# 64-token attention chunks from the fourth window on with reordered queues, and a first pair with one table set

## Chip, cores, metric

One core of a Trainium2 chip. The metric is the device time of a whole execution in microseconds (us). The profiler's span, from the first to the last instruction, is about 1.7 us shorter than the time of the same run in most runs, and all moments below are counted from the start of the span. Most executions agree within about 1%; runs marked slow (over 1.5% above the fastest of the same kernel) are left out of the ratios.

## The reference

A decayed linear attention over 64-token blocks, and behind it a layer norm, a two-layer MLP and a residual. B = 4, H = 8, S = 768, D = 64; the MLP is 512 to 2048 to 512.

```python
for b in range(nb):                       # 12 blocks of 64 tokens
    intra = einsum('bhic,bhjc->bhij', qb, kb) * Dmask
    intra = einsum('bhij,bhjd->bhid', intra, vb)
    inter = einsum('bhid,bhde->bhie', qb * lam_pow, kv_state)
    out[:, :, sl] = intra + inter
    kv_state = lam_block * kv_state + einsum('bhsd,bhse->bhde', kb * rev_pow, vb)
# ... x = out as (B, S, 512)
xn = (x - mean) / sqrt(var + 1e-6) * g_ln
out = x + relu(xn @ w_ch1) @ w_ch2
```

## The kernel before

The work is cut into 12 windows of 256 tokens (3 stretches of the sequence by 4 batches), numbered 0 to 11. A window gives the MLP two tiles of 128 tokens, one "group". The order of issue is written by hand: `plan` is the list of MLP steps (eight first-layer and eight second-layer steps for each group), and `add(n, ...)` hangs pieces of attention, of preparation and of transfers behind step n. SyncE (SP) issues the loads, the stores and the transposes by DMA, all in one queue. POOL (GpSimd) prepares K, Q and V of each window (`p0`) and decays the state.

Windows below LB use 128-token chunks, those from LB on use 64-token chunks, with less arithmetic. The two layouts differ in how a load is cut: two neighbouring tokens are 512 contiguous bytes, one token is 256.

```python
LB = 6

def source(src, u, hs):                   # u < LB: packets of 512 B, one DMA
    return src[b, hs, cc * W:(cc + 1) * W, :].rearrange("h (p j) d -> p h (j d)", j=2)
def fill(got, name, u, hs):               # u >= LB: packets of 256 B, two DMAs
    for j in range(2):
        nc.sync.dma_start(got[:, hs, j * D:(j + 1) * D],
                          src[b, hs, cc * W + j * C:..., :].rearrange("h p d -> p h d"))
# ...
def p0(u, k_eng=None):                    # preparation: POOL
    open_window(u)
    in_k(u, k_eng or nc.gpsimd)
    in_q(u, nc.gpsimd)
    in_v(u, nc.gpsimd)

def states64(u, j):                       # the state chain of a 64-token window (shortened)
    nc.vector.tensor_tensor(mid, s["pk"][0][:, j], old, op=ALU.add)     # Smid, VectorE
    nc.vector.tensor_tensor(tmp, s["pk"][1][:, j], mid, op=ALU.add)     # Stmp, VectorE
    decay(nc.gpsimd, Sn, tmp)                                           # Sn, POOL
    nc.gpsimd.tensor_copy(Sm, mid)                                      # Sm, POOL

def X(u):                                 # end of window u-1, front of window u (shortened)
    av64(u - 1); inter(u - 1, 0); kv64(u); scores64(u); inter(u - 1, 1)
    states64(u, 0); mask64(u, 0); states64(u, 1)
    norm(u - 1, 0); norm(u - 1, 1); mask64(u, 1)
# ...
add(12, (s4, 2), (p4, 2), (p0, 3, nc.vector), (transpose_dma, 3))
add(25, (s1, 3)); add(27, (s2, 3)); add(29, (s3, 3)); add(30, (s4, 3), (p4, 3))
for n, name in zip((30, 31, 32), "kqv"):
    add(n, (load_one, 6, name))
add(38, (s1, 4))
add(39, (p0, 6))                          # preparation of window 6, before ...
# ...
add(50, (s1, 5), (rstd_of, 4))            # ... window 5's state
```

`norm(u)` leaves the input xc of the MLP, and `p4(u)` has it transposed by DMA into xT; the group of window u starts on TensorE when xT is there.

## Time and profile before

| | before |
|---|---|
| time, median of 3 runs | 215.92 us (214.59 to 216.27) |
| span, granted TensorE clock | 214.9 us, 0.996 |
| starts of groups 2, 3, 4, 5, 6 on TensorE | 55.02, 72.02, 89.93, 106.11, 121.47 us |

The prediction below shows the page, the windows and the chain. What it does not show, and what decided the case, is the order of POOL's work around window 6. The timeline of POOL of the kernel before; its columns are start, duration, engine and line, operation, output <- inputs with their sizes, count, and in brackets the idle time just before with what ended it:

```profile
74.00 0.61 POOL L287 TENSOR_TENSOR Sn<-Stmp,lam_s 128x256 bf16<-128x256 f32 x1 [5.34 <-DVE Stmp L291]
...
75.70 1.16 POOL L199 CAST kq<-kin 128x512 bf16<-128x512 f32 x2
77.58 2.23 POOL L210 TENSOR_TENSOR kq<-qin,lam_p 128x512 bf16<-128x512 f32 x2 [0.72 <-DMA qin<-in_q_dram]
80.48 1.90 POOL L216 TENSOR_TENSOR vb<-vin,lam_p 128x1024 bf16<-128x1024 f32 x1 [0.67 <-DMA vin<-in_v_dram]
87.22 0.61 POOL L287 TENSOR_TENSOR Sn<-Stmp,lam_s 128x256 bf16<-128x256 f32 x1 [4.85 <-DVE Stmp L291]
```

At 74.00 POOL decays a state of window 4, from 75.70 to 82.4 it prepares window 6, whose loads are there (it waits 0.72 us for Q and 0.67 us for V), and at 87.22 it decays a state of window 5. So the order that will matter, window 6's preparation ahead of window 5's decays, is already in this kernel. POOL comes 4.85 us early to the last line. It has room, but only because window 6's loads are early.

### The profile page before, as it was taken

The page shows a single profiled execution, that of the slowest core. Times are in us where ns is not written, and L with a number is a line of the kernel's source. Part 1 is how long each engine was busy: PE and PEld are TensorE (multiplying, and loading weights), DVE is VectorE, ACT ScalarE, POOL GpSimd, SP SyncE. Part 2 cuts the span into 40 slices and gives each one's busy share as a digit, 9 for nine tenths or more (in the row PEclk, how much of TensorE's full clock was granted, in tenths as well). Part 3 has the DMA queues.
Part 4 walks back from the last instruction along what each step waited for, and adds up shares of the span by engine and source line. Part 5 has one row for each costly group of instructions (what it writes and reads, how often), then busy time and mean ns, then how long its engine had stood idle before and what let it go on. Part 6 is the DMA issues. An engine that isn't in the chain of part 4 may idle for free.

```text
span 214.9 us, 6642 instructions
## 1 busy us (share of the span) xinstructions
PE 201.9 (94%) x2884; PEld 138.2 (64%) x2899; DVE 102.9 (48%) x225; ACT 87.1 (41%) x165; POOL 79.4 (37%) x111
## 2 busy tenths in 40 slices
PE   2989999999799999999999999999999999999992
PEld 0568788454674675585585685784784874866861
DVE  3678461565168436747347256174183292522011
ACT  4765679120442244055063162261370460731600
POOL 4747139039464173229019138056065020000000
PEclk9999999999999999999999999999999999999998
DMA  4999999999999898799799999998998511320303
GB/s 130 289 272 207 219 263 160 236 284 234 215 303 208 169 229 153 110 215 209 126 220 199 137 230 200 177 203 198 206 246 131 128 27 27 99 52 0 98 3 95
DMA packets 94142, 37.13 MB, mean 173 GB/s; under 512 B 68385, under 2 KB 91169, under 8 KB 94114
## 3 DMA queue, kind: packets, MB, share of 16 engines
q1 hardware_dynamic: 89584, 32.38, 71.4%
q0 software_dynamic: 4224, 4.19, 12.4%
q8 instruction: 22, 0.36, 0.7%
q10 hardware_dynamic: 306, 0.14, 0.3%
q14 instruction: 6, 0.05, 0.1%
HBM read 27.27 MB, written 6.29 MB: 156 GB/s over the span
## 4 chain that ended last, share of the span: by engine, by line
PE 75%; DMA 13%; POOL 4%; SPq 3%; DVE 2%; issue 1%; POOLq 0%
PE pm L484 35%; PE pm L522 30%; DMA vin<-in_v_dram 6%; DMA qin<-in_q_dram 4%; SPq L71 3%; DMA kqT<-kq 2%; POOL kq L210 2%; POOL vb L216 2%; PE pm2h L513 2%; PE po L406 1%; PE po L393 1%; PE sc L247 1%; PE po L380 1%; PE sc L327 1%; PE pm1t L496 1%
## 5 line engine op out<-in xcount | busy, mean ns | idle before, releaser
L487 ACT ACTIVATE hT<-pm 128x512 bf16<-128x512 f32 x92 | 54.9, 601 | 91.2 <-PE pm L484 91.0
L484 PE MATMUL pm<-xT,w 128*128 128x256 bf16 x736 | 86.3, 273 | 1.9 <-DMA xT<-xc 1.2
L522 PE MATMUL pm<-w,hT 128*128 128x512 bf16 x353 | 81.1, 379 | 1.0 <-issue 0.3
L484 PEld LDWEIGHTS <-w 128*128 128x128 bf16 x736 | 69.8, 98 | 13.8 <-DMA xT<-xc 1.7
L522 PEld LDWEIGHTS <-hT 128*128 128x128 bf16 x368 | 35.5, 98 | 40.0
L543 DVE SCALAR_TENSOR_TENSOR o<-pm,rstd,x 128x512 f32<-128x512 f32 x23 | 17.1, 748 | 43.5 <-PE pm L522 43.4
L287 POOL TENSOR_TENSOR Sn<-Stmp,lam_s 128x256 bf16<-128x256 f32 x16 | 9.7, 611 | 69.7 <-DVE Stmp L365 49.0
L435 DVE SCALAR_TENSOR_TENSOR xc<-po,mv,g_row 128x512 bf16<-128x512 f32 (+1 forms) x24 | 16.8, 706 | 1.8
L257 DVE TENSOR_TENSOR mA<-sc,keep 128x512 bf16<-128x512 f32 x20 | 13.1, 685 | 6.8 <-PE sc L247 6.7
L428 ACT COPY x<-po 128x512 f32<-128x512 f32 x18 | 9.9, 588 | 11.3 <-PE po L393 5.3
L430 DVE BATCH_NORM_STATS2 stats<-x 128x6 f32<-128x512 f32 x18 | 12.4, 688 | 3.9 <-ACT x L428 3.9
L417 DVE COPY seen<-po 128x8 f32<-128x8 f32 x18 | 2.3, 162 | 23.2 <-PE po L406 23.2
L216 POOL TENSOR_TENSOR vb<-vin,lam_v 128x1024 bf16<-128x1024 f32 (+1 forms) x7 | 11.8, 1696 | 3.7 <-DMA vin<-in_v_dram 3.7
L210 POOL TENSOR_TENSOR kq<-qin,lam_q 128x512 bf16<-128x512 f32 x10 | 10.3, 1045 | 7.0 <-DMA qin<-in_q_dram 7.0
L210 POOL TENSOR_TENSOR kq<-qin,lam_p 128x512 bf16<-128x512 f32 x12 | 12.3, 1042 | 0.9 <-DMA qin<-in_q_dram 0.7
L216 POOL TENSOR_TENSOR vb<-vin,lam_p 128x1024 bf16<-128x1024 f32 x6 | 11.4, 1896 | 1.7 <-DMA vin<-in_v_dram 1.7
L199 POOL CAST kq<-kin 128x512 bf16<-128x512 f32 (+1 forms) x18 | 10.3, 599 | 0.6 <-DMA kin<-in_k_dram 0.6
L333 DVE TENSOR_TENSOR mA<-sc,keep 128x512 bf16<-128x512 f32 x12 | 8.2, 681 | 1.4 <-PE sc L327 1.4
L406 PE MATMUL po<-Sn,kqT 64*64 64x64 bf16 x216 | 7.4, 199 | 0.0
L224 PE MATMUL tp<-ident,kq 128*128 128x128 bf16 x48 | 6.2, 277 | 0.3 <-ACT kq L199 0.2
L406 PEld LDWEIGHTS <-kqT 64*64 64x64 bf16 x304 | 5.3, 108 | 1.5 <-issue 1.5
L224 PEld LDWEIGHTS <-kq 128*128 128x128 bf16 x48 | 4.1, 120 | 3.2 <-DVE kq L199 1.5
(98 smaller groups left out, 146.0 us busy)
## 6 DMA issues: line engine op xcount, KB each, us to landing
out_dram<-o SPq DMA_DIRECT2D x22, 256.0 KB, 4.5
w<-in_moe_w_ch_dram POOLq DMA_DIRECT2D x8, 512.0 KB, 9.6
kin<-in_k_dram SPq DMA_DIRECT2D x14, 256.0 KB, 3.9
qin<-in_q_dram SPq DMA_DIRECT2D x14, 256.0 KB, 5.2
vin<-in_v_dram SPq DMA_DIRECT2D x14, 256.0 KB, 5.6
kin<-in_k_dram SPq DMA_DIRECT2D x5, 512.0 KB, 6.5
qin<-in_q_dram SPq DMA_DIRECT2D x5, 512.0 KB, 8.7
vin<-in_v_dram SPq DMA_DIRECT2D x5, 512.0 KB, 7.7
```

Source lines behind the costliest of these rows:

```text
L199: (eng.copy if eng is nc.scalar else eng.tensor_copy)(dst[:, :, :, j], src[:, :, :, j])
L210: eng.tensor_tensor(dst[:, :, :, j], src[:, :, :, j], lq[:, :, :, j:j + 1].to_broadcast([128, n, 2, D]), op=ALU.mult)
L216: eng.tensor_tensor(st[u]["vb"][:, hs], qkv_in[u]["v"][:, hs], lv.to_broadcast([128, n, 2, D]), op=ALU.mult)
L224: nc.tensor.transpose(tp[:, i, j, :], s["kq"][:, a, p, j], ident)
L257: nc.vector.tensor_tensor(s[f"mA{hf}"][:, e], s[f"sc{hf}"][e], kp[:, None, :, :].to_broadcast([128, 2, 2, 128]), op=ALU.mult)
L406: nc.tensor.matmul(s["po"][ab][half[jq], 2 * p + e, :], lhsT=qT[half[e], p, jq, half[ab]], rhs=s["S"][ab][jq][half[e], p, :], start=False, ...
L430: nc.vector.bn_stats(stats, po if early else x)
L435: nc.vector.scalar_tensor_tensor(xc[:, sl], in0=po[:, sl], scalar=mv[:, 0:1], in1=g_row[:, sl], op0=ALU.subtract, op1=ALU.mult)
L484: nc.tensor.matmul(pm[:, b, :], lhsT=w1[n // W2K][:, kk, (n % W2K) * 128:(n % W2K + 1) * 128], rhs=xT_of[g][:, kk, 0:N], start=(b == 0 and ...
L487: nc.scalar.activation(hT[:, u * NB:(u + 1) * NB, 0:N], pm, ACT.Relu)
L522: nc.tensor.matmul(acc[i], lhsT=hT[:, kk, i * 128:(i + 1) * 128], rhs=w2[kk // W2K][:, kk % W2K, :], start=(kk == 0), stop=(kk == KB - 1))
L543: nc.vector.scalar_tensor_tensor(o[:, ab], in0=a, scalar=rstd[:, ab:ab + 1], in1=x[:, ab], op0=ALU.mult, op1=ALU.add)
```

## The change

Three intents. Windows 3, 4 and 5 take the 64-token form too (LB from 6 to 3), so TensorE has less attention to do. The queues are reordered for that: window 4's K on another queue, its Q and V behind window 2's transposes, the stores of windows 0 to 2 taken out of the MLP's finish and issued later, K and Q transposes issued one by one. In the first pair, one table set with Ln and Exp is loaded up front, and copies and scores are moved forward.

```diff
-    LB = 6
+    LB = 3
+    nc.scalar.preload_act_table_set("natural_log_exp_and_others")
-        elif ab == 1:
-            for j in range(2):
-                nc.sync.dma_start(rows[j], o[half[j]])
+        elif ab == 1 and u > 2:
+            store(u)
     # ... first pair: order of transposes, copies and activations (cut)
+    def first64(u, ahead=None):
+        kv64(u)
+        scores64(u)
+        if ahead is not None:
+            in_q_one(ahead, nc.gpsimd, 0)
+        mask64(u, 0)
+        states64(u, 0)
+        if ahead is not None:
+            in_q_one(ahead, nc.vector, 1)
+        mask64(u, 1)
+        states64(u, 1)
     # ... the plan; the old entries of windows 3 to 5 are taken out
+    add(11, (open_window, 3), (in_k, 3, nc.scalar), (in_q, 3, nc.gpsimd))
+    add(12, (s4, 2), (make_keep64,), (in_v, 3, nc.gpsimd), (load_one, 4, "k", nc.scalar))
+    add(12, (transpose_dma, 3, 0), (to_xT, 2, 0), (transpose_dma, 3, 1), (to_xT, 2, 1))
+    add(12, (load_one, 4, "q"), (load_one, 4, "v"))
+    add(20, (open_window, 4), (in_k, 4, nc.vector))
+    add(21, (first64, 3, 4))
+    add(22, (transpose_dma, 4, 0), (transpose_dma, 4, 1), (load_one, 5, "k"), (load_one, 5, "q"))
+    add(23, (in_v, 4, nc.gpsimd))
+    add(28, (wind_up, 3), (p4, 3), (load_one, 5, "v"))
+    add(28, (open_window, 5), (in_k, 5, nc.gpsimd), (transpose_dma, 5, 0))
+    add(30, (first64, 4))
+    add(32, (in_q, 5, nc.gpsimd), (in_v, 5, nc.gpsimd))
+    add(34, (rstd_of, 3), (transpose_dma, 5, 1), (store, 0), (store, 1))
+    add(40, (store, 2))
-    for j in range(6, NU):
+    for j in range(5, NU):
         at = 55 + 16 * (j - 6)
-        if j > 6:
-            for n, name in zip((23, 21, 19), "kqv"):
+        if j > 5:
+            for n, name in zip((17, 16, 15) if j == 6 else (23, 21, 19), "kqv"):
                 add(at - n, (load_one, j, name))
             add(at - 13, (p0, j))
     # ... transposes one by one; the old entries of the block X (cut)
+        add(at + (4 if j == 5 else 2), (X, j), (p4, j - 1))
```

With j = 6, the loads of window 6 stand at steps 38 to 40 and its preparation at step 42. Window 5's block `X` stands at step 39 + 4 = 43. In the kernel before the loads stand at steps 30 to 32, the preparation at 39 and window 5's first state at 50: the change issues the loads eight steps later and the block seven steps earlier.

More of the change, by code (lines that the diff above doesn't have):

```diff
@@ L66, in source, with fill @@
         return src[b, hs, cc * W:(cc + 1) * W, :].rearrange("h (p j) d -> p h (j d)", j=2)
-    def fill(got, name, u, hs):
+    def fill(got, name, u, hs, eng=None):
+        eng = eng or nc.sync
         src = dict(k=k, q=q, v=v)[name]
         if u < LB:
-            nc.sync.dma_start(got[:, hs], source(src, u, hs))
+            eng.dma_start(got[:, hs], source(src, u, hs))
             return
@@ L74, in fill, with load_one @@
         for j in range(2):
-            nc.sync.dma_start(got[:, hs, j * D:(j + 1) * D],
-                              src[b, hs, cc * W + j * C:cc * W + (j + 1) * C, :].rearrange("h p d -> p h d"))
-    def load_one(u, name):
+            eng.dma_start(got[:, hs, j * D:(j + 1) * D],
+                          src[b, hs, cc * W + j * C:cc * W + (j + 1) * C, :].rearrange("h p d -> p h d"))
+    def load_one(u, name, eng=None):
         got = inp.tile([128, H, 2 * D], F32, tag=name + "in", name=name + "in")
-        fill(got, name, u, slice(0, H))
+        fill(got, name, u, slice(0, H), eng)
         qkv_in.setdefault(u, {})[name] = got.rearrange("p h (j d) -> p h j d", j=2)
@@ L148 @@
     nc.vector.memset(eps_t, eps)
+    nc.vector.tensor_copy(e_p[:, 0:1], io_p)
+    nc.vector.tensor_scalar(e_p[:, 1:2], e_p[:, 0:1], -1.0, None, op0=ALU.mult)
     e_q = const.tile([128, 1], F32)
@@ L211, in in_q, with in_q_one @@
                               lq[:, :, :, j:j + 1].to_broadcast([128, n, 2, D]), op=ALU.mult)
+    def in_q_one(u, eng, j):
+        src = qkv_in[u]["q"].rearrange("p (a e) j d -> p a e j d", e=2)
+        lq = lam_p[:, 0, :].rearrange("p (a e) -> p a e", e=2)
+        eng.tensor_tensor(part(1, st[u]["kq"], ALL)[:, :, :, j], src[:, :, :, j],
+                          lq[:, :, :, None].to_broadcast([128, NP, 2, D]), op=ALU.mult)
     def in_v(u, eng, hs=ALL):
@@ L225, in transpose_pe, with transpose_dma @@
         (eng.tensor_copy if eng else nc.scalar.copy)(s["kqT"][:, a, pairs[0]:pairs[0] + n], tp)
-    def transpose_dma(u):
+    def transpose_dma(u, a):
         s = st[u]
-        s["kqT"] = wk.tile([128, 2, NP, 2, 128], BF16, tag="kqT", bufs=3, name="kqT")
-        for a in range(2):
-            nc.sync.dma_start_transpose(s["kqT"][:, a].rearrange("p b j t -> p (b j) t"),
-                                        s["kq"][:, a].rearrange("p b j e d -> p (b j e d)"))
+        if "kqT" not in s:
+            s["kqT"] = wk.tile([128, 2, NP, 2, 128], BF16, tag="kqT", bufs=3, name="kqT")
+        nc.sync.dma_start_transpose(s["kqT"][:, a].rearrange("p b j t -> p (b j) t"),
+                                    s["kq"][:, a].rearrange("p b j e d -> p (b j e d)"))
     def scores(u, hf, early=False):
@@ L268, in mask_by_act, with mask_two_ways @@
             nc.vector.tensor_tensor(m, m, kp[:, None, :, :].to_broadcast([128, 2, 2, 128]), op=ALU.mult)
+    def mask_two_ways(u, hf):
+        s = st[u]
+        m = s[f"mA{hf}"][:, 1]
+        nc.scalar.copy(m, s[f"sc{hf}"][1])
+        mask(u, hf, (0,))
+        kp = keep_h.rearrange("p a b t -> p a (b t)")
+        nc.vector.tensor_tensor(m, m, kp[:, None, :, :].to_broadcast([128, 2, 2, 128]), op=ALU.mult)
     def kv(u, tag="mm"):
@@ L452, in to_xT @@
         else:
-            xt = mm_tile([128, KA, 128], BF16, "xt")
-            for kk in range(KA):
-                nc.tensor.transpose(xt[:, kk, :], s["xc"][:, ab, kk * 128:(kk + 1) * 128], ident)
-            nc.scalar.copy(dst, xt)
+            n_x = 2 if t == 0 else 1
+            for i_x in range(n_x):
+                w = KA // n_x
+                xt = mm_tile([128, w, 128], BF16, "xt")
+                for kk in range(w):
+                    at = i_x * w + kk
+                    nc.tensor.transpose(xt[:, kk, :], s["xc"][:, ab, at * 128:(at + 1) * 128], ident)
+                (nc.vector.tensor_copy if i_x else nc.scalar.copy)(dst[:, i_x * w:(i_x + 1) * w], xt)
     def rstd_of(u):
@@ L547, in finish, with store @@
                 nc.sync.dma_start(rows[j][:, ab], o[half[j], ab])
-        elif ab == 1:
-            for j in range(2):
-                nc.sync.dma_start(rows[j], o[half[j]])
+        elif ab == 1 and u > 2:
+            store(u)
+    def store(u):
+        for j in range(2):
+            nc.sync.dma_start(rows_of(u)[j], o_of[u][half[j]])
     def finish_half(t, a, z, w):
@@ L589 @@
     load_window(1)
-    in_k(0, nc.vector, HA)
-    transpose_pe(0, 0, (0, 1))
-    keep_busy(1, "po0")
     for j in range(2):
@@ L597 @@
         nc.scalar.activation(lam_s[half[e]], ln_p[half[e], :, e], ACT.Exp, scale=float(C))
+    in_k(0, nc.vector, HA)
+    transpose_pe(0, 0, (0, 1))
     nc.vector.tensor_tensor(lam_q[:, :, 1], lam_q[:, :, 0], lam_b, op=ALU.mult)
-    nc.vector.tensor_copy(e_p[:, 0:1], io_p)
-    nc.vector.tensor_scalar(e_p[:, 1:2], e_p[:, 0:1], -1.0, None, op0=ALU.mult)
-    for i in range(2):
-        nc.scalar.activation(lam_p[:, i], lnlam, ACT.Exp, scale=e_p[:, i:i + 1])
     in_q(0, nc.vector, HA)
@@ L609 @@
     transpose_pe(0, 0, (2, 3), nc.vector)
+    scores(0, 0)
+    transpose_pe(0, 1, (2, 3))
     nc.scalar.copy(g_row, g_all)
-    transpose_pe(0, 1, (2, 3))
+    for i in range(2):
+        nc.scalar.activation(lam_p[:, i], lnlam, ACT.Exp, scale=e_p[:, i:i + 1])
     sqrt_first = const.tile([128, 1], F32)
@@ L614 @@
     in_v(0, nc.gpsimd, HB)
-    scores(0, 0)
     mask(0, 0)
     scores(0, 1, early=True)
-    mask_by_act(0, 1)
+    mask_two_ways(0, 1)
     kv(0)
@@ L644, in m1s @@
             f(u)
-    transpose_pe(1, 0, (0, 1), nc.vector)
-    transpose_pe(1, 0, (2, 3), nc.vector)
     to_xT(0, 0)
@@ L653 @@
     m1a.tile(0, 0)
+    transpose_pe(1, 0, (0, 1), nc.vector)
+    transpose_pe(1, 0, (2, 3), nc.vector)
     to_xT(0, 1)
@@ L694 @@
     load_window(3, after_pool=True)
-    load_window(4)
     def p0(u, k_eng=None):
@@ L748, in wind_up @@
                 odd = xh[:, :, 1 - ab]
-                nc.vector.tensor_tensor(odd, odd, rest[ab].rearrange("p (a e) d -> p a e d", e=2)[:, :, 1 - ab], op=ALU.add)
+                rows = slice(0, 128) if s["S"][ab][0] is not None else half[1]
+                nc.vector.tensor_tensor(odd[rows], odd[rows], rest[ab].rearrange("p (a e) d -> p a e d", e=2)[rows, :, 1 - ab], op=ALU.add)
             stats = wk.tile([128, 6], F32, tag="stats", name="stats")
@@ L852 @@
     add(10, (s3, 2))
-    add(12, (s4, 2), (p4, 2), (p0, 3, nc.vector), (transpose_dma, 3))
-    for n, name in zip((14, 15, 16), "kqv"):
-        add(n, (load_one, 5, name))
+    add(11, (open_window, 3), (in_k, 3, nc.scalar), (in_q, 3, nc.gpsimd))
+    add(12, (s4, 2), (make_keep64,), (in_v, 3, nc.gpsimd), (load_one, 4, "k", nc.scalar))
+    add(12, (transpose_dma, 3, 0), (to_xT, 2, 0), (transpose_dma, 3, 1), (to_xT, 2, 1))
+    add(12, (load_one, 4, "q"), (load_one, 4, "v"))
     add(15, (rstd_of, 2))
-    add(17, (p0, 4))
@@ L858 @@
-    add(25, (s1, 3))
-    add(25, (transpose_dma, 4))
-    add(27, (s2, 3))
-    add(28, (p0, 5))
-    add(29, (s3, 3))
-    add(30, (s4, 3), (p4, 3))
-    for n, name in zip((30, 31, 32), "kqv"):
-        add(n, (load_one, 6, name))
-    add(34, (rstd_of, 3), (make_keep64,))
-    add(37, (transpose_dma, 5))
-    add(38, (s1, 4))
-    add(39, (p0, 6))
-    add(40, (s2, 4))
-    add(42, (s3, 4))
-    add(44, (s4, 4), (p4, 4))
-    add(46, (transpose_dma, 6))
-    add(50, (s1, 5), (rstd_of, 4))
-    add(53, (s2, 5))
@@ L877 @@
+    add(40, (store, 2))
+    for j in range(5, NU):
         at = 55 + 16 * (j - 6)
-        if j > 6:
-            for n, name in zip((23, 21, 19), "kqv"):
+        if j > 5:
+            for n, name in zip((17, 16, 15) if j == 6 else (23, 21, 19), "kqv"):
                 add(at - n, (load_one, j, name))
             add(at - 13, (p0, j))
-            add(at - 8, (transpose_dma, j))
-        if j < LB:
-            add(at, (s1_s3, j))
-            add(at + 4, (s2_s4, j), (p4, j - 1))
-        else:
-            if j == 6:
-                add(at + 1, (X1, j))
-                add(at + 5, (X2, j), (p4, j - 1))
-            else:
-                add(at + 2, (X, j), (p4, j - 1))
+            add(at - 8, (transpose_dma, j, 0), (transpose_dma, j, 1))
+        add(at + (4 if j == 5 else 2), (X, j), (p4, j - 1))
```

## The prediction

> **What bounds the kernel now.** I read the page first, then the windows view cut at the starts of the MLP groups, then the chain of waits in order of time, then the timeline. The page:
>
> ```profile
> span 214.9 us, 6642 instructions
> PE 201.9 (94%) x2884; PEld 138.2 (64%) x2899; DVE 102.9 (48%) x225; ACT 87.1 (41%) x165; POOL 79.4 (37%) x111
> ```
>
> TensorE is the bound, so time can only come from less work on it, or from its 13 us of idleness. The windows view of TensorE (start:end, length, busy, clock, DMA share, GB/s), cut where groups 2, 3, 4, 5, 6 and 7 of the MLP start:
>
> ```profile
> 55.02:72.02 17.00, 16.57 (x239) 1.00 0.98 222
> 72.02:89.93 17.91, 17.66 (x319) 1.00 0.97 178
> 89.93:106.11 16.18, 15.91 (x258) 1.00 0.89 178
> 106.11:121.47 15.36, 15.31 (x225) 1.00 1.09 188
> 121.47:136.69 15.22, 15.17 (x217) 1.00 1.03 197
> ```
>
> A group of two 128-token tiles costs 15.22 to 15.36 us beside one 64-token window, and 16.2 to 17.9 us in the stretch where windows 3, 4 and 5 run with 128-token chunks. That stretch is what the main part of the change attacks. The start, from the chain of waits (start, length, what):
>
> ```profile
> 7.58 12.64 DMA vin<-in_v_dram
> 20.22 0.07 issue
> 20.29 1.91 POOL vb L216
> 22.20 0.04 issue
> 22.24 0.45 PE pk L281 x32
> ```
>
> The first path that counts is not the first pair's arithmetic. It is the load of V for window 1, which lands at 20.22, its scaling on POOL, and the state matmuls at 22.24. [...] nothing behind 22.24 moves unless that load moves.
>
> Last, three lines of the timeline: TensorE waiting ahead of group 2, and inside a steady group the weight load that waits for VectorE to read the state banks.
>
> ```profile
> 55.02 1.25 PE L484 MATMUL pm<-xT,w 128*128 128x256 bf16 x10 [1.20 <-DMA xT<-xc]
> 112.16 0.42 DVE L362 TENSOR_TENSOR Smid<-pk,Sn 128x256 f32<-128x256 f32 x1
> 112.64 1.42 PEld L484 LDWEIGHTS <-w 128*128 128x128 bf16 x14 [0.19 <-DVE Smid L362]
> ```
>
> [...] loads at 1.84, 4.50 and 20.55, each 1.28 us; the one at 4.50 goes. [...] between 41 and 45 us, loads in 512 B packets move 305 GB/s with the DMA full, and between 122 and 127 us, in 256 B packets, 215 GB/s. [...] 16 first-layer matmuls of 128 columns take 1.86 us at 15.82 and 1.05 us at 18.85.
>
> **Part 1, the first pair.** Removed: a 1.28 us table load ahead of lam_q, the dummy matmul of 0.63 us, two lam_p activations (0.50 us) from ahead of a copy. Window 0's first scores move up by about 0.6 us, but Q's second half lands at 7.77 and its scaling takes 0.76 us, so the second scores stay near 10. One mask is read from PSUM while ScalarE copies the other; with g_row and lam_p now ahead of that copy it ends where it ended, about 12.2. Splitting the first transposed copy between ScalarE and VectorE saves 0.3 to 0.5 us before the first MLP matmul at 15.82. All of it is ahead of 22.24, where V of window 1 releases the queue. The DMA share from 10 to 20 us is full, the weight chunk that released the matmul at 20.77 arrives just before, and the weight triggers on POOL are unchanged. **Worth on the end: 0**, at best 0.3 us.
>
> **Part 2, less attention on TensorE.** From the chain of waits of window 3: scores 0.42 + 0.35 and AV 0.64; of a 64-token window: scores 0.29, AV 0.38. Saved per window 0.48 + 0.26 = 0.74, less 0.1 for eight more state matmuls (eight take 0.13 with their switch), so 0.65; for three windows 2.0 us. There are fewer switches too: a block of 16 MLP matmuls takes 1.75 us undisturbed and 1.85 after each attention piece, and the new schedule has one or two pieces per window instead of four or five. To get both together I use the groups. MLP alone is 15.25 - 1.28 (one 64-token window: 0.38 + 0.13 + 0.32 + 0.29 + 0.16) = 13.97. From group 2 to group 5 the old kernel takes 17.00 + 17.91 + 16.18 = 51.09. The new one needs 3 x 13.97 = 41.9, the end of window 3 (0.38 + 0.13 + 0.13 = 0.64), the front of window 4 (0.32 + 0.29 = 0.61), two full windows (2.56): 45.7, with 0.4 for switches 46.1. The front of window 3, 0.7, moves ahead of group 2. Difference 51.1 - 46.1 - 0.7 = **4.3 us**.
>
> **Part 3, the queues.** Window 4's load no longer stands ahead of window 2's transposes (K goes on ACT's queue, Q and V behind them). Window 2's transposes were issued from 49.08 although their first input was there at 46.1; so the 1.20 us wait at 55.02 should go, partly because 0.7 us of window 3 now fills it. **1.2 us at most.** But load 3 now has 256 B packets: 1.5 MB at 215 rather than 305 GB/s is 7.0 against 4.9 us, about 2 us later at the end of V (it was scaled from 49.06). V of window 3 is then ready near 53 to 54.4, just when TensorE wants it at 53.84, and the second transpose of window 2 lands at 54 to 55.5. I give back **0.7** of the 1.2.
>
> **Part 4, new waits.** The state tiles of a 64-token window take two of the four "mm" PSUM buffers; the third MLP step after needs the first back. In the steady group TensorE does two steps (1.75 us) and then waits 0.19. Ahead of group 2 the VectorE queue is longer: finish of tile 3 (0.75, from 53.85), mask 0.68, two state ops 0.84, half of Q of window 4 (0.68 by the masks' size), mask 0.68, state op 0.42. From the end of the scores about 3.4 us, against 1.75 us of MLP work: **1.6 us** of stall, more if Q of window 4, loaded behind the transposes, lands later than about 56. I estimate 56 to 57.3, so another 0.3. At window 4 its scores need the two "sc" buffers in which the end of window 3 has its rest terms; VectorE frees the second after ScalarE's copy 0.6, add 0.42, stats 0.69, aggregate 0.18, xc 0.75, add 0.41 = 3.05 us, and TensorE comes after two steps, 0.32 of state matmuls and the rest terms, some 2.2: **0.8 us**. Small frictions 0.2.
>
> Sum: 4.3 + 1.2 - 0.7 - 1.6 - 0.3 - 0.8 - 0.2 = **1.9 us**; a less tight queue ahead of group 2 gives 2.9. I take 2.5. On the quoted median of 215.92 that is 213.4 us, and a little of chance improvement in the first 22 us makes it **213.2**.
>
> **Rivals.**
> - *The waits are hidden.* If Q of window 4 lands early and VectorE overlaps more, parts 2 and 3 come through whole: 5 us, 210.9. For it: the author placed these pieces by hand. Against: the VectorE sum above, and the 0.19 us wait that the steady group already shows.
> - *DMA becomes the bound from 45 to 75.* Its share is already 0.97 to 0.98 there, and windows 3 to 5 get slower packets. Then V of window 3 and Q of window 4 come two or more microseconds late, TensorE stalls 3 to 4 us around 54 to 60, and the time is 215 to 216. For it: the 305 against 215 GB/s. Against: window 4's load and the stores of windows 0 to 2 leave that stretch.
> - *The start counts after all.* If the first pair's shorter chain let MLP work run ahead of 22.24, up to 1 us more: 212. Against: V of window 1 and the weights. [...]
>
> **Range and chances.** The full gain gives 210.9, the DMA rival 216. Eight in ten: 211.0 to 215.4. Faster by over 2% needs 4.3 us, nearly all of parts 2 and 3 without a new stall: 0.2. Slower by over 2% needs a broken queue: 0.02. Within: 0.78.
>
> **What would show it.** Right: the state matmuls of window 1 still start at 22.0 to 22.4, released by V's load; the group before group 2 ends near 53.8; TensorE has a wait of 1 to 2 us on VectorE's state op at the third MLP step of group 2 and one of 0.5 to 1 us in front of window 4's scores; groups 3 and 4 take 15.3 to 15.5 us; from group 5 on nothing differs but the shift. Wrong: a start that moves, or group 2 and the front of window 4 without waits (then near 211), or waits on the loads of window 3 or 4 of over 2 us (then 215 or more).

## The result

| | before | after |
|---|---|---|
| time, median of 4 runs | 215.54 us (214.59 to 216.27) | 231.25 us (229.45 to 232.85) |
| span, clock | 214.9 us, 0.996 | 228.2 us, 0.976 |
| group 2 starts | 55.02 | 55.91 (+0.9) |
| group 3 starts | 72.02 | 73.74 (+1.7) |
| group 4 starts | 89.93 | 101.31 (+11.4) |
| group 5 starts | 106.11 | 118.43 (+12.3) |
| group 6 starts | 121.47 | 134.84 (+13.4) |

The outputs are correct. The ratio of fast runs is 1.072, with a 95% interval of 1.064 to 1.0801: **the changed kernel is 7.2% slower**. Ratios here are the mean time of one kernel's fast runs over that of the other's of the same rounds, so not quite the ratio of the medians quoted beside them.

The page of the kernel after: the span, the busy times, then TensorE's busy share and granted clock in tenths, in 40 slices of 5.7 us:

```profile
span 228.2 us, 6498 instructions
PE 200.7 (88%) x2810; PEld 138.1 (61%) x2810; DVE 103.8 (45%) x228; ACT 85.9 (38%) x165; POOL 80.0 (35%) x115
...
PE   1879999998879996029999899999999999999993
...
PEclk9999999999999999758999999999999999999999
```

There is one hole, in slices 16 to 18 counted from 1, from 15 x 5.7 = 85.6 us on (6, 0, 2), and the clock falls in slices 17 to 19 (7, 5, 8). Nearly everything else is as full as before. The windows view of TensorE of the kernel after, cut where groups 2 to 7 start (start:end, length, busy, clock, DMA share, GB/s):

```profile
55.91:73.74 17.83, 15.77 (x216) 1.00 1.00 182
73.74:101.31 27.57, 15.61 (x226) 0.87 0.68 144
101.31:118.43 17.12, 17.12 (x226) 0.90 1.12 181
118.43:134.84 16.41, 15.52 (x226) 1.00 0.94 193
134.84:150.06 15.22, 15.22 (x219) 1.00 1.10 199
```

Set against the prediction's five rows of before, the stretches differ by +0.8, +9.7, +0.9, +1.1 and 0.0 us; with the +0.9 in front of them that is the whole 13.4 us. Two things are seen here. The stretch before group 4 has 15.61 us of work in 27.57, so TensorE stood idle for 12.0 us of it (0.25 before), while its work fell by 17.66 - 15.61 = 2.05. And the stretch behind it is fully busy for 17.12 us at a clock of 0.90: a slow array counts as busy, so the busy column hides it and the clock column shows it. The timeline of TensorE at the start of group 2 of the kernel before, then at the start of group 4 of the kernel after:

```profile
55.02 3.65 PE L484 MATMUL pm<-xT,w 128*128 128x256 bf16 x32 [1.20 <-DMA xT<-xc]
```

```profile
101.31 5.25 PE L507 MATMUL pm<-xT,w 128*128 128x256 bf16 x32 [11.96 <-DMA xT<-xc]
```

The same number of matmuls takes 1.6 us more; the granted clock is 0.50 from 101.31 to 104.00 (1.00 from 55.02 to 58.67 in the kernel before). This is what the expectations below call a half-rate stretch. The wait is for the transposed xc of window 4. It leads back through VectorE. Its timeline in the kernel after:

```profile
94.52 0.42 DVE L381 TENSOR_TENSOR Smid<-pk,Sn 128x256 f32<-128x256 f32 x1 [12.81 <-POOL Sn L306]
```

VectorE stood for 12.81 us in window 5's state chain, which `X` puts ahead of window 4's norm, waiting for a decay on POOL. POOL's timeline in the kernel after:

```profile
85.26 0.61 POOL L203 CAST kq<-kin 128x512 bf16<-128x512 f32 x1 [7.28 <-DMA kin<-in_k_dram]
...
87.17 2.04 POOL L214 TENSOR_TENSOR kq<-qin,lam_p 128x512 bf16<-128x512 f32 x2 [0.38 <-DMA qin<-in_q_dram]
92.02 1.90 POOL L226 TENSOR_TENSOR vb<-vin,lam_p 128x1024 bf16<-128x1024 f32 x1 [2.80 <-DMA vin<-in_v_dram]
93.87 0.61 POOL L306 TENSOR_TENSOR Sn<-Stmp,lam_s 128x256 bf16<-128x256 f32 x1
```

The decay at 93.87 waited for nothing of its own. It stood behind window 6's preparation, and that stood for 7.28 + 0.38 + 2.80 us (and 0.30 at the second half of K) waiting for window 6's loads. The queue of SyncE shows why those were late; here "us" is how long the issuing instructions held the queue:

```profile
71.57 4.73 SPq L241 DMA_TRANSPOSE kqT<-kq  x2
76.35 3.20 SPq L576 DMA_DIRECT2D out_dram<-o  x4
79.60 2.59 SPq L76 DMA_DIRECT2D kin<-in_k_dram  x2
82.23 2.69 SPq L76 DMA_DIRECT2D qin<-in_q_dram  x2
85.02 1.36 SPq L576 DMA_DIRECT2D out_dram<-o  x2
86.42 2.41 SPq L76 DMA_DIRECT2D vin<-in_v_dram  x2
97.09 2.86 SPq L470 DMA_TRANSPOSE xT<-xc  x2
```

Window 6's loads stand behind the transposes of window 5 and behind the stores that the change moved here. So the chain is: stores and transposes, loads of window 6, its preparation on POOL, window 5's decay, window 4's norm, its transposes (97.09), TensorE (101.31), and then a slow array. Window 6 itself needs none of this until a group later.

Three smaller waits of TensorE are in the timeline too: 0.57 us for window 3's transposes at 55.30, and these two:

```profile
60.44 2.78 PE L507 MATMUL pm<-xT,w 128*128 128x256 bf16 x24 [0.82 <-DVE Smid L381]
...
67.31 0.44 PE L346 MATMUL sc<-kqT 64*64 64x64 bf16 x31 [1.23 <-DVE x L784]
```

### The profile page after: what moved, and what is told of

It reads as the page before. It is cut to its first block, busy times and chain, and to the rows that moved or that the text cites. A ratio compares the mean times of both kernels' runs of the same rounds, so it can differ in the third digit from the quotient of the medians.

```text
span 228.2 us, 6498 instructions
## 1 busy us (share of the span) xinstructions
PE 200.7 (88%) x2810; PEld 138.1 (61%) x2810; DVE 103.8 (45%) x228; ACT 85.9 (38%) x165; POOL 80.0 (35%) x115
## 3 DMA queue, kind: packets, MB, share of 16 engines
q0 software_dynamic: 4224, 4.19, 11.4%
## 4 chain that ended last, share of the span: by engine, by line
PE 71%; DVE 8%; DMA 7%; SPq 6%; POOL 3%; ACT 2%; issue 2%; ACTq 0%; DVEq 0%; POOLq 0%
PE pm L507 31%; PE pm L545 27%; SPq L76 3%; DMA qin<-in_q_dram 2%; PE pm1t L519 2%; DMA vin<-in_v_dram 2%; SPq L576 2%; DMA g_one<-in_moe_g_ln_dram 2%; PE tp L234 2%; PE pm2h L536 2%; DVE stats L449 1%; DVE xc L454 1%; PE po L425 1%; PE po L399 1%; DMA xT<-xc 1%
## 5 line engine op out<-in xcount | busy, mean ns | idle before, releaser
L507 PE MATMUL pm<-xT,w 128*128 128x256 bf16 x736 | 87.2, 276 | 13.8 <-DMA xT<-xc 12.1
L507 PEld LDWEIGHTS <-w 128*128 128x128 bf16 x736 | 71.2, 99 | 26.2 <-issue 14.5
L226 POOL TENSOR_TENSOR vb<-vin,lam_p 128x1024 bf16<-128x1024 f32 x9 | 17.1, 1898 | 4.9 <-DMA vin<-in_v_dram 4.8
L214 POOL TENSOR_TENSOR kq<-qin,lam_p 128x512 bf16<-128x512 f32 x16 | 16.4, 1044 | 2.6 <-DMA qin<-in_q_dram 2.6
L454 DVE SCALAR_TENSOR_TENSOR xc<-po,mv,g_row 128x512 bf16<-128x512 f32 (+1 forms) x22 | 15.3, 702 | 1.6
L381 DVE TENSOR_TENSOR Smid<-pk,Sn 128x256 f32<-128x256 f32 x17 | 7.2, 423 | 14.4 <-POOL Sn L306 12.8
L352 DVE TENSOR_TENSOR mA<-sc,keep 128x512 bf16<-128x512 f32 x18 | 12.3, 681 | 0.7 <-PE sc L346 0.7
L484 ACT ACTIVATE std<-mv,eps_t 128x2 f32<-128x2 f32 x12 | 3.6, 299 | 19.3 <-DVE mv L450 16.4
L389 POOL CAST Sm<-Smid 128x256 bf16<-128x256 f32 x18 | 7.6, 425 | 1.0 <-DVE Smid L381 1.0
L267 DVE TENSOR_TENSOR mA<-sc,keep 128x512 bf16<-128x512 f32 x8 | 5.2, 686 | 5.1 <-PE sc L257 5.1
L168 PE MATMUL g_all<-g_one,ones 1*128 1x512 f32 x2 | 2.0, 1120 | 5.1 <-DMA g_one<-in_moe_g_ln_dram 5.1
L346 PE MATMUL sc<-kqT 64*64 64x64 bf16 x288 | 4.8, 195 | 1.8 <-DVE x L784 1.2
```

The lines of the kernel that those rows point to most:

```text
L214: eng.tensor_tensor(dst[:, :, :, j], src[:, :, :, j], lq[:, :, :, j:j + 1].to_broadcast([128, n, 2, D]), op=ALU.mult)
L226: eng.tensor_tensor(st[u]["vb"][:, hs], qkv_in[u]["v"][:, hs], lv.to_broadcast([128, n, 2, D]), op=ALU.mult)
L352: nc.vector.tensor_tensor(s["mA"][:, e], s["sc"][e], keep64[:, None, None, :].to_broadcast([128, NP, 2, D]), op=ALU.mult)
L454: nc.vector.scalar_tensor_tensor(xc[:, sl], in0=po[:, sl], scalar=mv[:, 0:1], in1=g_row[:, sl], op0=ALU.subtract, op1=ALU.mult)
L507: nc.tensor.matmul(pm[:, b, :], lhsT=w1[n // W2K][:, kk, (n % W2K) * 128:(n % W2K + 1) * 128], rhs=xT_of[g][:, kk, 0:N], start=(b == 0 and ...
```

## The experiments

Twelve kernels ran, all with correct outputs. "Ratio" is against the kernel before in the same rounds.

| run | built on | ratio [95%] | median, us |
|---|---|---|---|
| e1_prep6_behind_x5 | after | 1.0323 [1.0233, 1.0414] | 223.04 |
| e2_load6_early | after | 1.0401 [1.032, 1.0482] | 224.53 |
| e3_stores_behind_load6 | after | 1.0623 [1.0548, 1.0698] | 228.54 |
| e4_first_pair_only | before | 1.0021 [0.9961, 1.0081] | 215.87 |
| e5_order_mended | after | 1.0305 [1.0222, 1.0387] | 221.25 |
| e6_chunks_alone | before | 1.0314 [1.0243, 1.0384] | 222.29 |
| e7_two_orders | after | 1.0322 [1.0254, 1.0391] | 222.64 |
| e8_mended_stores_earlier | after | 1.013 [1.0041, 1.022] | 220.43 |
| e9_small_packets_only | before | 1.0221 [1.013, 1.0313] | 221.81 |
| e10_chunks_queue_mended | before | 1.0441 [1.0377, 1.0505] | 225.68 |
| e11_mended_transposes_first | after | 1.0194 [1.0081, 1.0307] | 222.05 |
| e12_chunks_from_window5 | before | 1.0035 [0.9969, 1.0101] | 217.78 |

e1 to e7 ran on one chip, e8 to e12 on another. The profiles of e1, e8 and e11 fell in the slow state: they are read for the order of events only, and the ratios come from the fast runs. Medians are of all runs.

**Theory**: the loss is one queue order on POOL, fed by late loads of window 6. **Rival**: the 64-token windows cost it by themselves, through transfers in 256-byte packets.

### e1: the preparation of window 6 behind window 5's block

```diff
-            add(at - 13, (p0, j))
+            if j > 6:
+                add(at - 13, (p0, j))
+        if j == 5:
+            add(at + 4, (p0, 6))
```

> The changed kernel with one line of schedule moved: POOL's preparation of window 6 (its K, Q and V conversions) stands behind window 5's attention block in program order instead of one step ahead of it. My theory (order on POOL: the state decay of window 5 stands behind work that waits for window 6's loads, VectorE waits 12.8 us for that decay, the norm of window 4 stands behind VectorE): the 12.0 us wait of TensorE ahead of group 4 goes, and with it most of the half-rate stretch after it (32 matmuls in 5.25 instead of 3.5 us); profiled span about 214 to 216, a ratio to before of 0.99 to 1.01. Rival (the load of window 6 is simply too late, whatever stands behind what): the wait moves ten us on, in front of window 6's own block, and the span stays above 222.

The loss falls from 7.2 to 3.2%: one moved line is worth 4 points, some 8 us in the medians (231.25 to 223.04). The expected ratio of 0.99 to 1.01 was missed. The timeline of TensorE of e1, then the queue of SyncE:

```profile
95.25 5.32 PE L507 MATMUL pm<-xT,w 128*128 128x256 bf16 x32 [3.77 <-DMA xT<-xc]
```

```profile
86.99 1.40 SPq L576 DMA_DIRECT2D out_dram<-o  x2
88.43 2.02 SPq L76 DMA_DIRECT2D vin<-in_v_dram  x2
90.55 3.33 SPq L470 DMA_TRANSPOSE xT<-xc  x2
```

Group 4 still waits 3.77 us, not 11.96, and again starts slowly. Now window 4's transposes themselves stand in SyncE's queue behind a store and window 6's V. So the wait of 12 us is shown to hang on POOL's order, and something is left.

### e2 and e3: the loads of window 6 earlier; the stores behind them

```diff
+    for name in "kqv":                                       # e2: at step 32
+        add(32, (load_one, 6, name))
-            for n, name in zip((17, 16, 15) if j == 6 else (23, 21, 19), "kqv"):
...
-    add(34, (rstd_of, 3), (transpose_dma, 5, 1), (store, 0), (store, 1))
-    add(40, (store, 2))
+    add(34, (rstd_of, 3), (transpose_dma, 5, 1))             # e3
+    add(48, (store, 0), (store, 1), (store, 2))
```

> The changed kernel with POOL's order as it is, but the loads of window 6 issued ahead of the last transpose of window 5 and of the three postponed stores. V of window 6 should land near 82 instead of 91.9. If the order on POOL makes the wait as long as the load is late, the wait of TensorE ahead of group 4 shrinks by about as much, to 1 to 4 us, and the span goes to 216 to 219; the transpose of Q of window 5 comes later, which may cost 1 to 2 us in front of window 5's scores. If the loads have nothing to do with it, the wait stays at 12.

> The changed kernel with the stores of windows 0, 1 and 2 moved behind the loads of window 6 in the queue, nothing else. The two groups of stores hold the queue for 3.2 and 1.36 us ahead of V of window 6. My theory: V lands 4 to 5 us earlier, TensorE's wait ahead of group 4 goes from 12.0 to 7 to 8 us, span about 223 to 224. If the stores are harmless to this wait: no change from 228.

The timeline of TensorE of e2, then of e3:

```profile
85.34 0.64 PE L346 MATMUL sc<-kqT 64*64 64x64 bf16 x32 [5.86 <-DMA kqT<-kq]
...
96.83 3.66 PE L507 MATMUL pm<-xT,w 128*128 128x256 bf16 x32
```

```profile
95.28 5.43 PE L507 MATMUL pm<-xT,w 128*128 128x256 bf16 x32 [6.42 <-DMA xT<-xc]
```

In e2 the wait ahead of group 4 is gone, as the theory has it: earlier loads alone remove it too, so it took both, late loads and POOL's order. But window 5's Q transpose, which the loads had overtaken, was issued only at 79.48, and TensorE waited 5.86 us for it at window 5's scores. The ratio, 1.0401, missed the expectation: the wait had moved. In e3 the wait ahead of group 4 fell from 11.96 to 6.42 us, so the stores made up 5.5 us of it. That hit the expected 7 to 8 roughly, but the total did not: the span fell by only 1.6 us, because the group still started slowly (5.43 us), the wait in group 2 was 1.54 us instead of 0.82, and two new waits followed, 1.49 us in group 4 and 1.75 us ahead of group 5. The first of these two is a fault of the edit, seen again in e7: with all three stores at step 48, VectorE waited 8.69 us for an output buffer.

### e4: the first pair alone

The whole first-pair part of the diff, on the kernel before.

> The kernel before with the first part of the change alone (the shorter chain of the first pair, one table set, no dummy matmul); chunks, loads and queues as before. My prediction said that it is worth nothing, because V of window 1 and the weights set the start of the state matmuls at 22.24. Expected: same, ratio 0.997 to 1.003. The changed kernel's trace shows group 1 0.5 us later than before, at 31.80 instead of 31.26; if that comes from this part, the ratio is 1.002 to 1.004; if the shorter chain counts, 0.995 or less.

Same time: 1.0021, with an interval of 0.9961 to 1.0081. The first MLP matmuls started at 15.71 us instead of 15.82 and the state matmuls of window 1 at 22.23 instead of 22.24. TensorE no longer waits for V there (0.42 us before): its own scores now come at 20.68 instead of 19.83, so the two chains end together.

### e6: the chunks alone, in the old kernel's order

```diff
-    LB = 6
+    LB = 3
     # ... add(25, (s1, 3)) and the like become add(25, (first64, 3)) and add(29, (s3c, 3))
```

> The kernel before with 64-token chunks from window 3 on and nothing else: its own queue order, its own steps, its own first pair. My sum gave 2.0 us for less work on TensorE and some for fewer switches. Expected: span 212 to 213.5, ratio 0.982 to 0.995. If the smaller packets of the loads of windows 3 to 5 make DMA the bound, as one rival had it: TensorE waits 2 us or more for window 3's or 4's inputs, ratio over 1.005.

Neither queue nor POOL order of the change is in e6, and it is 3.1% slower: the expectation was missed, and the rival's sign came. The timeline of TensorE of e6:

```profile
58.32 5.20 PE L484 MATMUL pm<-xT,w 128*128 128x256 bf16 x32 [4.46 <-DMA xT<-xc]
```

TensorE waited 4.46 us ahead of group 2 (1.20 before), and 1.83 us ahead of group 3. Window 2's transposes were issued at 53.38, not 49.08. So the 64-token windows cost something by themselves in this order; whether through their packets or their arithmetic, e9 tells.

### e9: the packets alone

The old kernel with its arithmetic and its layout, but windows 3 to 5 loaded as the change loads them, by two DMAs of 256-byte pieces each.

```diff
-            nc.sync.dma_start(got[:, hs], source(src, u, hs))
+            if u < 3:
+                nc.sync.dma_start(got[:, hs], source(src, u, hs))
+                return
+            rows = src[b, hs, ..., :].rearrange("h (p j) d -> j p h d", j=2)
+            for j in range(2):
+                nc.sync.dma_start(got[:, hs, j * D:(j + 1) * D], rows[j])
```

> The kernel before, with its 128-token chunks and its whole schedule, but the loads of windows 3, 4 and 5 cut into two each of 256 B runs in place of one of 512 B runs; the same bytes in the same places, the result right. The chunks alone lost 5 us: TensorE waited 4.46 us ahead of group 2 for window 2's transposes, which stood behind the loads of windows 3 and 4 in the queue (issued at 53.38 instead of 49.08). If the packets are the cause, this kernel has about the same wait ahead of group 2 (3.5 to 5 us) and a ratio of 1.02 to 1.04. If the 64-token arithmetic is the cause, ratio 0.998 to 1.005.

2.2% slower with nothing changed but the packets (and so the number of DMAs). The DMA view from 38 to 54 us, first of the kernel before, then of e9:

```profile
DMA packets 7823, 4.05 MB, mean 253 GB/s; under 512 B 1048, under 2 KB 7820, under 8 KB 7820
```

```profile
DMA packets 11875, 3.48 MB, mean 217 GB/s; under 512 B 11283, under 2 KB 11872, under 8 KB 11872
```

The same 16 us move 0.57 MB less. What that delays is seen in the queue of SyncE, first of the kernel before, then of e9:

```profile
49.08 3.64 SPq L451 DMA_TRANSPOSE xT<-xc  x2
```

```profile
37.95 5.54 SPq L77 DMA_DIRECT2D qin<-in_q_dram  x2
...
52.73 3.04 SPq L457 DMA_TRANSPOSE xT<-xc  x2
```

The loads of windows 3 and 4 hold the queue longer (15.8 us, not 12.2), and window 2's transposes, behind them, go out 3.7 us later, though their input was there at 48.4 in both. In the timeline of TensorE of e9:

```profile
57.64 5.32 PE L490 MATMUL pm<-xT,w 128*128 128x256 bf16 x32 [3.77 <-DMA xT<-xc]
```

Group 2 starts 57.64 - 55.02 = 2.6 us late and its first 32 matmuls take 5.32 - 3.65 = 1.7 us more: 4.3 of the 4.6 us by which the span grew (219.5 against 214.9). So a delay of 2.6 us costs 4.3, because the array runs slowly behind the wait: the granted clock is 0.91 from 54 to 72 us, where the kernel before has 1.00.

### e10: the chunks with the queue mended

e6 with window 4's loads behind window 2's transposes, and window 4's preparation and transposes at step 26.

```diff
-    load_window(4)
-    add(12, (s4, 2), (p4, 2), (make_keep64,), (p0, 3, nc.vector), (transpose_dma, 3))
+    add(12, (s4, 2), (p4, 2), (make_keep64,), (p0, 3, nc.vector), (transpose_dma, 3), (load_window, 4))
-    add(17, (p0, 4))
+    add(26, (p0, 4), (transpose_dma, 4))
```

> The chunks alone in the kernel before, with the load of window 4 moved behind window 2's transposes (as the change has it) and window 4's preparation on POOL behind window 3's block. Theory: the 4.46 us wait ahead of group 2 falls to 1 us or less [...]; span 213 to 216, ratio 0.99 to 1.01, the rest being window 3's or 4's own inputs. If the wait stays over 3 us, the loads of window 4 were not what held the transposes.

The wait ahead of group 2 went, as expected (group 2 at 55.29), but the total got worse, 4.4%. The timeline of TensorE of e10:

```profile
80.15 1.86 PE L484 MATMUL pm<-xT,w 128*128 128x256 bf16 x8 [8.64 <-DMA xT<-xc]
```

Window 3's transposes, whose input was there at 69.5, were issued at 76.22, behind the loads of 5 and 6, two stores and window 4's transposes. Mending one place of SyncE's queue moved the wait one group on.

### e5, e7, e8, e11: what the change is worth with the orders mended

e7 is e1 and e3 together. e5 is that, and window 5's Q is prepared and transposed at step 28, and window 4's Q stands behind window 3's masks and states:

```diff
-        if ahead is not None:
-            in_q_one(ahead, nc.gpsimd, 0)
         mask64(u, 0)
         # ...
         states64(u, 1)
+        if ahead is not None:
+            in_q_one(ahead, nc.gpsimd, 0)
+            in_q_one(ahead, nc.vector, 1)
...
-    add(28, (open_window, 5), (in_k, 5, nc.gpsimd), (transpose_dma, 5, 0))
+    add(28, (open_window, 5), (in_k, 5, nc.gpsimd), (in_q, 5, nc.gpsimd), (transpose_dma, 5, 0), (transpose_dma, 5, 1))
```

> The changed kernel with two moves alone: window 6's preparation on POOL behind window 5's block, and the stores of windows 0 to 2 behind the loads of window 6. With the first alone TensorE still waited 3.77 us ahead of group 4 for the transposes of window 4, which stood in the queue behind the loads of window 6 and two groups of stores (issued at 90.55, their input ready at 86.4). Theory: these moves together take that wait to 1 us or less [...]; span 216 to 219, what is left being the wait ahead of group 2 and in front of window 4's scores. If the queue has nothing to do with it, the 3.8 us stay and the span is 221 to 223.

> The changed kernel with its queues mended where the traces so far show work standing behind a later need: window 6's preparation on POOL behind window 5's block, the stores of windows 0 to 2 behind the loads of window 6, window 5's Q ahead of window 4's state decays on POOL with its transpose right behind, and window 4's Q behind the masks and states of window 3. If the loss is all order on POOL and on the SP queue: no wait of TensorE over 1 us behind group 2's start, group 4 starts at 87 to 89, span 211 to 214 (the gain that I had predicted), ratio 0.98 to 0.995. If the 64-token windows 3 to 5 lose by themselves (256 B packets, more POOL work), it stays over 217.

In both, group 4 starts without a wait, at 89.20 us in e7 and 88.56 in e5; the kernel before has 89.93. Up to there the chunks pay in these profiles. But both missed what was expected of them (ratios 1.0322 and 1.0305; spans of 221.0 and 218.8 us, which is where the texts put them if the theory were wrong), through a fault of my own. The timelines of VectorE and of TensorE of e7:

```profile
95.76 1.41 DVE L566 SCALAR_TENSOR_TENSOR o<-pm,rstd,x 128x512 f32<-128x512 f32 x2 [9.07 <-DMA out_dram<-o]
```

```profile
96.66 0.64 PE L365 MATMUL pk<-vb,kq 64*64 64x64 bf16 x32 [3.26 <-DVE o L566]
...
97.87 5.73 PE L507 MATMUL pm<-xT,w 128*128 128x256 bf16 x32
```

There are three output buffers. With all three stores at step 48, VectorE waited 9.07 us to write the fourth, and TensorE 3.26 us for VectorE, with a slow stretch behind it. e8 is e5 with the stores where they can no longer do that:

```diff
-    add(48, (store, 0), (store, 1), (store, 2))
+    add(42, (store, 0), (store, 1))
+    add(48, (store, 2))
```

> The mended order again, with one mistake of mine undone: in it the stores of windows 0 to 2 stood so late that VectorE waited 8.3 us for an output buffer and TensorE 2.51 us for VectorE ahead of window 6's states, with 32 matmuls at half rate after it (5.33 instead of 3.7 us). Here the stores of windows 0 and 1 follow the loads of window 6 at once, where the queue stood idle from 79.9 to 83.7. Expected: that wait and its half-rate stretch go, about 4 us; span 214 to 216, ratio 0.995 to 1.01. If they stay, something else holds window 6.

The best form of the change, and still 1.3% slower than before (1.0041 to 1.022; two fast runs, 219.26 and 218.22): the expected 0.995 to 1.01 was missed. The wait and the slow stretch at window 6 did go (32 matmuls in 3.67 us at 97.65). The profile, of a slow run, shows what came instead. The queue of SyncE, then the timeline of TensorE of e8:

```profile
82.34 4.97 SPq L576 DMA_DIRECT2D out_dram<-o  x4
87.42 3.44 SPq L470 DMA_TRANSPOSE xT<-xc  x2
```

```profile
92.26 3.65 PE L507 MATMUL pm<-xT,w 128*128 128x256 bf16 x32 [1.73 <-DMA xT<-xc]
```

The two halves of window 4's xc were ready at 85.5 and 87.2, and the transposes stood behind the stores until 87.42. The two slow runs had a granted clock of 0.992 and the two fast ones 1.0; the profiled slow run has a slow stretch in group 2 (56 matmuls in 7.48 us at 57.27, where e5 takes 6.32; a clock of 0.6 to 0.7 in the page's slice from 55.0 to 60.5; behind a wait of 2.33 us). If such stretches are what makes them slow, leaving them out flatters e8; that is not shown.

e11 is e8 with window 2's second transpose ahead of window 3's, and window 3's block at step 23:

```diff
-    add(12, (transpose_dma, 3, 0), (to_xT, 2, 0), (transpose_dma, 3, 1), (to_xT, 2, 1))
+    add(12, (transpose_dma, 3, 0), (to_xT, 2, 0), (to_xT, 2, 1), (transpose_dma, 3, 1))
-    add(21, (first64, 3, 4))
+    add(23, (first64, 3, 4))
```

> As the mended order with earlier stores, and besides both of window 2's transposes ahead of the transpose of window 3's Q, with window 3's block two MLP steps later. In the mended order TensorE waited 1.64 us ahead of group 2 for the second of those transposes. Expected: that wait falls to 0.5 us or less; 0.5 to 1.5 us faster than the kernel of the same call without it, span 213 to 215.

1.0194, with an interval that overlaps e8's: no gain is shown, so the expectation was missed, and two fast runs each can't tell them apart. The wait ahead of group 2 did go in e11's profile (a slow run), and others took its place: 1.54 us for VectorE ahead of group 3, 1.80 ahead of group 4 and 2.19 ahead of group 5.

### e12: 64-token chunks from window 5 only

The loads of windows 3 and 4 keep their 512-byte packets, and only window 5 is changed (LB = 5, its front at step 50, window 6's block in one piece).

> The kernel before with 64-token chunks from window 5 on instead of from window 6 on, with its own queues: windows 3 and 4, whose loads share the full DMA queues with the last weights and with window 2's transposes, keep their 512 B packets. Theory (small packets hurt only where a transpose that TensorE waits for stands behind them): no new wait ahead of group 2 (1.2 us as before), at most 0.6 us more ahead of group 3, and window 5's block costs 0.7 us less, with fewer switches; ratio 0.992 to 1.002, so perhaps a version that beats both. If 64-token chunks cost by themselves, ratio over 1.005.

Same time, 1.0035 (0.9969 to 1.0101, 5 rounds). The timeline of TensorE of e12:

```profile
74.49 1.03 PE L484 MATMUL pm<-xT,w 128*128 128x256 bf16 x8 [2.88 <-DMA xT<-xc]
```

A wait of 2.88 us ahead of group 3 was not expected (0.6 at most was): window 3's transposes were issued at 70.62, not 68.18, behind window 5's load, a store and window 4's transposes. From group 3 to group 5 it then takes 107.36 - 74.49 = 32.87 us where the kernel before takes 105.94 - 72.02 = 33.92 in the same view (the 106.11 above is from the chain of waits): 1.05 us are gained for one window, 0.86 of it in busy time, and window 6's block in one piece is part of that. So the chunks do what they are for, and the loads take it back. No version here beats the kernel before.

## Why the prediction was wrong

It said 213.2 us, within 2%. It was 231.25. A slowdown of over 2%, which "needs a broken queue", had been given two chances in a hundred, and a broken queue is what came.

- **Part 1, the first pair, 0: right in size.** e4 shows no change within its interval, and in the kernel after the state matmuls start at 22.11. That V's load holds them was right of the kernel before only; in e4 and in the kernel after TensorE does not wait for it.
- **Part 2, 4.3 us less on TensorE: the right mechanism, nearly twice too large.** From the end of group 1 to the start of group 5 TensorE is busy for 49.99 us in the kernel before and 49.23 in the kernel after, of which 1.6 are the slow stretch: 2.4 us less. e5 gives the same (49.26 - 1.68 = 47.58). The 51.09 of the sum is the length of three stretches and holds 0.95 us in which TensorE stood idle, and the 46.1 set against it is 46.7 when measured (48.34 - 1.6, from 55.91 to 118.26). The prediction's own plainer figure, 2.0 us for three windows, was near. With 2.4 in place of 4.3 its four parts sum to zero: no gain was left, even without the wait.
- **Part 3, the queues, 1.2 - 0.7: right at its own place, too small as a whole.** The 1.20 us ahead of group 2 did become 0.17 and 0.57. But I priced the small packets as a load 3 that ends 2 us later, and charged 0.7. By themselves they cost 4.6 us of span (e9). The missing steps: the loads, issued longer (15.8 us, not 12.2), held the transposes behind them in the same queue (issued at 52.73, not 49.08), and the array ran slowly behind the wait of 3.77 us that followed (32 matmuls in 5.32 us, not 3.65). The slower packets themselves were not missed. In e9 all traffic moved more slowly by a factor of 253 / 217 = 1.17 from 38 to 54 us. The prediction had taken more, 305 / 215 = 1.42; its 215 comes from a window, 122 to 127 us, in which the DMA is not full throughout (its share falls to 0.3).
- **Part 4, new waits, 1.6 + 0.3 + 0.8: both occurred, in other sizes.** 0.82 us on VectorE's state op, at the fifth step and not the third, and 1.23 us at window 4's scores: 2.05 together.
- **The step that failed: that the stores leave the crowded stretch and no other wait comes.** Against the DMA rival I wrote that "window 4's load and the stores of windows 0 to 2 leave that stretch", and in the last part that groups 3 and 4 take 15.3 to 15.5 us. The stores did leave. They went to 76.35, ahead of the loads of window 6, where they made up 5.5 us of the wait (e3). Window 6's loads were early enough for window 6, whose block did not wait for them at 106.88. What the prediction leaves out is what stands behind window 6's preparation on POOL: at step 42 it comes before window 5's block at step 43, and so a late load of window 6 stops window 5's decay, VectorE, window 4's norm and TensorE for 12 us. e1, which changes this alone, brings the loss from 7.2 to 3.2%. The sign that the text named for being wrong, a wait of over 2 us on the loads of window 3 or 4, is not what came.
- **The slow stretch after a wait.** My text had slow matmuls at the start of the kernel (16 in 1.86 us at 15.82 against 1.05 at 18.85, both at a granted clock of 1.00, so what slowed them is not shown), but none behind the stall of 3 to 4 us in the DMA rival. A slow stretch added 1.6 us behind group 4's wait (32 matmuls in 5.25 us, not 3.65), and as much in e1, e6 and e9 (5.32, 5.20 and 5.32). Behind the waits that I did allow for, 0.82 and 1.23 us, the matmuls ran at the usual speed (24 in 2.78 us at 60.44, 31 for scores in 0.44 at 67.31).
- **The DMA rival** named the right evidence and bounded it too low, at 216; the small packets alone give 221.81.

Of the 7.2%, then, e1 shows 4 points to hang on POOL's order; e2, which moves window 6's loads instead, brings back 3.2. Of the 3.2 left, e9 shows that the packets alone cost 2.2 in the old kernel; that it is the same 2.2 in the new one is argued, not shown. **Open**: a gap of 0.89 us ahead of matmuls at 126.14 that the profile puts down to no wait, present in most variants of the change (0.66 to 0.94 us; in e10 a gap of 0.86 us at that place is put down to VectorE's state op) and absent in the kernel before, e3, e9 and e12; how much of e8's 1.3% is the packets and how much the queue order that is left; and whether e11 differs from e8.

## What to carry to other kernels

When work is moved in a hand-ordered program, read for each queue what now stands behind every item that can wait, not only whether the item comes in time for its own user. The smaller transfers of e9 were a cost to what was issued behind them in the same queue (window 2's transposes, at 52.73 us and not 49.08), so price a transfer size there. And count a long wait of TensorE with a slow stretch on top: from group 2 to group 5, behind each wait of 3.26 us or more in these profiles, the next matmuls lost 1.5 to 2.1 us. Shorter waits went both ways: slow behind 2.51 us (e5: 32 matmuls in 5.33 us) and 2.19 (e11: 5.32), not behind 2.88 (e12: 8 in 1.03 us, as behind 0.62 in e9).

## Waits and the clock, loads and the queue

- Behind waits of 3.77, 4.46 and 11.96 us (e9, e6 and the kernel after) 32 matmuls took 5.32, 5.20 and 5.25 us, against 3.65 in the kernel before. The shorter waits do not go by their length: in e11 a wait of only 2.19 us, with MLP matmuls on both sides of it, was followed by 32 matmuls in 5.32 us (3.65 us at 91.43 in the same profile, one of a slow run), with a clock of 0.7 to 0.8 in the page's slice from 110.6 to 116.1; and in e5, a fast run, 2.51 us (with attention matmuls before and after) by 5.33 us, at a clock of 0.85 from 94 to 98. After 2.88 us (e12) no slice of the page shows a clock under 0.9, and that of the whole run is 1.00.
- How long the issue of a load held SyncE's queue while many transfers were under way bore on this case: at nearly the same place, the issue of one window's Q held it for 0.54 us as one DMA of 512-byte packets (before, at 37.23) and for 5.54 us as two of 256-byte packets (e9, at 37.95). In the kernel before the next issue, V's, took 4.42 us instead, so part of this is only a shift: all loads of windows 3 and 4 together hold the queue for 12.2 us (36.76 to 48.98) before and for 15.8 us (36.85 to 52.63) in e9.
